# A fused attention and expert kernel: logits of the last pass in twelve products of their own, rows by transposes, two turns moved

## The chip, the cores and the metric

The kernel runs on one core of a Trainium2 chip. Its time is device microseconds (us) of one execution, and what is quoted for a kernel is the median of several. A profiled execution is a further, single one; its trace gives the start and length of every instruction. The engines are TensorE (PE, with its weight loads as PEld), VectorE (DVE), ScalarE (ACT), GpSimd (POOL) and SyncE (SP, which here only issues transfers). Each engine runs its own instructions in the order in which they stand in its queue, and a semaphore holds an instruction until what it needs is there.

## The reference

Three stages follow each other on 1152 tokens (2 batches of 576) of 512 numbers. The first two stages make the tokens that the third one routes:

```python
x = attention_with_rotary(q, k, v)            # 2 x 8 heads x 576 x 64 -> 1152 x 512
h = x @ w_in;  g = h / (1 + exp(-1.702 h));  x = g @ w_out     # d_ff = 2048
logits = x @ w_gate                            # 8 experts
e = argmax(logits);  gate = softmax(logits)[e]
for i in range(1152):                          # slots in order of the tokens
    if counts[e[i]] < capacity: disp[e[i], counts[e[i]]] = x[i]; counts[e[i]] += 1
y = relu(disp @ w1[e]) @ w2[e]                 # F = 1024
out[i] = gate[i] * y[e[i], pos[i]]             # 0 for a token without a slot
```

## The kernel before

**Stages.** Attention comes first and is not touched. What the code calls the first part is the dense layer (`first`, L731): the tokens go through it in three passes of 480, 384 and 288 (`CUTS = 0, 5, 9, 12`, in blocks of 96 tokens, six blocks to a batch). The second part (`second`, L995, and `few`, L1018) is the experts' layer. It works on items: an item is up to 288 tokens of one expert, and a table `etab` says which expert. Items 0 and 1 hold tokens of batch 0 (3 blocks of 96, 2 of 112), items 2 and 3 those of batch 1 (3 of 96, 1 of 96), and for these inputs there are no more.

**Both layers** go through `ffn` (L690): weights arrive in slices, ACT (L672) and DVE (L673) split each into a high and a low part (`hl`, a ring of four buffers), twelve products make the hidden block `h` (L686), ACT and DVE turn it into `gh` and `gl`, and two slices later twelve products add to the output `y` (L712). A `hook` is a pair: a number of slices before the end, and a call to be made there.

**End of a pass of the first part** (L747 to L767). ACT copies `y` to `yt`, in which a column is a token. For each block of 96 tokens two tiles in PSUM are filled by products of `yt` with `turner`, which holds the identity beside the 512 x 8 gate weights: 128 columns of each product are the tokens' rows, 8 are partial logits. DVE copies the rows (L762), adds up the logits (L763, L766), and SP stores the rows in `x2` in DRAM (L767). The six tiles share two buffers of the pool `ps_m`.

**Routing** (`route`, L769) starts when the six blocks of a batch have logits. DVE finds each token's expert, PE counts tokens ahead of each with small products (`rank`, `count`, L815 to L824), DVE makes the slot number of each token (`r_at`, L856), and POOL scatters six lists of 96 entries into `slots` in DRAM (L868). `gather` (L936) then loads an item's entries (`ent`, L940) and gathers its tokens' rows from `x2` (`got`, L945, four buffers). `turn` (L955) transposes the gathered rows on PE (`tg`, L963) into the next item's input `xt`. Results leave with one scatter for each block (`out`, L987), on POOL's queue too.

**Order.** The program order above goes to a scheduler that places instructions by its own estimates; from then on each engine's order is fixed. The wait of one instruction holds up all behind it on its engine.

Of the kernel before, what the change touches and what calls it, by code (L numbers as in the profile page):

```python
# [9 lines left out]
F32 = mybir.dt.float32  # L10
# [14 lines left out]
P = 128  # L25
DM = H * D
ND = DM // P
N = B * S
DFF = 2048
E = 8  # L30
F2 = 1024
TT = 96
NT = S // TT
# [54 lines left out]
CUTS = 0, 5, 9, 12  # L88
# [505 lines left out]
class Experts:  # L594
# [137 lines left out]
    def first(self, k0, k1, hook=None):  # L732

        nc = self.nc
        nf = DFF // P

        def get(f):
            w = self.weights
            if f not in self.seen and f >= EARLY:
                for u in w.units(f):  # L740
                    u()
            self.seen.add(f)
            return self.halves(w.f[f])

        w = (k1 - k0) * TT
        y = self.ffn(self.xt[:, :, :, k0 * TT:k1 * TT], [lambda f=f: get(f) for f in range(nf)], self.gated, hook)
        yt = self.two.tile([P, ND, WIDE], F32, name="yt", bufs=1)  # L747
        for j in range(ND):
            nc.scalar.activation(out=yt[:, j, 0:w], in_=y[j][:, 0:w], func=AF.Copy)
        for k in range(k0, k1):  # L750
            b, i = divmod(k, NT)
            cs = slice((k - k0) * TT, (k - k0 + 1) * TT)
            row = self.three.tile([P, DM], F32, name="row")[0:TT]
            lg = self.three.tile([TT, 2, E], F32, name="lg", bufs=2)
            for n in range(2):
                t = self.ps_m.tile([P, 2, P + E], F32, tag="m", name="tr")
                for j in range(2):
                    nc.tensor.matmul(  # L758
                        t[0:TT, j], yt[:, 2 * n + j, cs], self.turner[:, 2 * n + j], start=True, stop=True
                    )  # L760
                out = row[:, n * 2 * P:(n + 1) * 2 * P].rearrange("p (j c) -> p j c", j=2)
                nc.vector.tensor_copy(out=out, in_=t[0:TT, :, 0:P])  # L762
                nc.vector.tensor_reduce(  # L763
                    out=lg[:, n], in_=t[0:TT, :, P:].rearrange("p j e -> p e j"), axis=AX.X, op=ALU.add
                )
            nc.vector.tensor_tensor(out=self.logits[b][:, i, :], in0=lg[:, 0], in1=lg[:, 1], op=ALU.add)  # L766
            nc.sync.dma_start(out=self.x2[b][i * TT:(i + 1) * TT, :], in_=row)  # L767

    def route(self, b, L):  # L769
# [66 lines left out]
        tt(sq, sq, items.unsqueeze(1).to_broadcast(wide), ALU.mult)  # L836
        red(base, sq)
        ts(at0, base, float(HALF), ALU.mult, float(first), ALU.add)
        red(ni, items)

# [212 lines left out]
    def run(self):  # L1053
        nc, tc = self.nc, self.tc
        sp = [mybir.EngineType.SP]
        found, x = {}, {}

        def turn(i):
            x[i] = self.turn(found[i][1], i)

        self.logits = [self.two.tile([TT, NT, E], F32, name=f"logits{b}", bufs=1) for b in range(B)]
        for n, (k0, k1) in enumerate(zip(CUTS, CUTS[1:])):
            self.first(k0, k1, {0: (10, self.setup), len(CUTS) - 2: (0, lambda: turn(0))}.get(n))
            if n == 0:
                self.clear()
            for b in range(B):
                if k0 < (b + 1) * NT <= k1:
                    self.route(b, self.logits[b])
                    for k in range(2 * b, 2 * b + 2):
                        found[k] = self.gather(k, [b], *STATIC[k])  # L1070
        for i in range(3):
            self.second(found[i][0], x[i], self.expert(i, sp), ((2, 0, 2)[i], lambda: turn(i + 1)))
        self.few(found[3][0], x[3], self.expert(3, sp))
        n = nc.values_load(self.etab[0:1, ITEMS:ITEMS + 1], min_val=4, max_val=ITEMS)
        with tc.For_i(4, n, 1) as i:
            ent, rows = self.gather(i, [0, 1])
            self.cut = []
            self.second(ent, self.turn(rows, 0), self.expert(i, sp))
# [30 lines left out]
```

## Time and profile before

| | us |
|---|---|
| median of 3 runs | 509.21 (508.87 to 510.66) |
| profiled execution | 510.11 |
| its span, first to last instruction | 508.3 |
| TensorE busy in the span | 469.7 (92%) |
| VectorE / ScalarE / GpSimd busy | 366.7 / 271.6 / 115.0 |
| mean granted TensorE clock | 0.983 |

Times inside a trace are counted from the span's start. The clock is a share of full speed; its two levels are 0.5 (1.2 GHz) and 1 (2.4 GHz), and a stretch's figure is a mean over it. A long share of busy time says little on where a microsecond could be saved: for that one looks for stretches in which the busiest engine stands still, and for what ended them.

### The profile page before, as it was taken

How to read it: one execution, taken by the hardware profiler on the slowest of the kernel's cores; microseconds unless marked ns; L12 is line 12 of the kernel's file. 1: busy time of each engine (PE TensorE's matmuls, PEld its weight loads, DVE VectorE, ACT ScalarE, POOL GpSimd, SP SyncE). 2: the span in 40 equal slices, each digit the busy share in tenths (PEclk: the TensorE clock that was granted, in tenths of full speed). 3: DMA queues.
4: the chain of work that ended last, by engine and by line, in shares of the span. 5: the costliest groups of instructions: out<-in, count | busy, mean ns of one | idle time of the engine just before them, and what ended most of it. 6: DMA issues, size and time to landing. Idle time of an engine off the chain costs nothing.

```text
span 508.3 us, 8728 instructions
## 1 busy us (share of the span) xinstructions
PE 469.7 (92%) x3206; PEld 421.6 (83%) x3206; DVE 366.7 (72%) x746; ACT 271.6 (53%) x514; POOL 115.0 (23%) x117
## 2 busy tenths in 40 slices
PE   1789999998999999999999999999999999499992
PEld 1777687687787778788899999999999999499991
DVE  6798999888788998999835534457856689355570
ACT  3577686676565733534563444466566455254640
POOL 5965633422211200000000000000444025601020
PEclk9999999999999999999999999999999999699997
DMA  7032322330224357574101240001076436735410
GB/s 256 1 100 75 99 77 74 99 80 26 53 64 155 105 187 254 188 265 177 41 1 31 63 170 1 0 11 55 2 250 206 132 125 195 246 97 191 162 50 14
DMA packets 20125, 55.63 MB, mean 109 GB/s; under 512 B 3685, under 2 KB 4869, under 8 KB 20080
## 3 DMA queue, kind: packets, MB, share of 16 engines
q1 hardware_dynamic: 17920, 50.91, 31.3%
q0 software_dynamic: 1728, 3.62, 2.4%
q8 instruction: 27, 0.44, 0.4%
q10 hardware_dynamic: 432, 0.51, 0.3%
q14 instruction: 18, 0.15, 0.1%
HBM read 43.86 MB, written 6.66 MB: 99 GB/s over the span
## 4 chain that ended last, share of the span: by engine, by line
PE 61%; DVE 16%; DMA 10%; issue 5%; ACT 4%; POOL 1%; SPq 0%; POOLq 0%; DVEq 0%; ACTq 0%
PE h L686 22%; PE y L712 20%; PE s L393 6%; PE pv L493 4%; DMA qx<-qs 3%; PE tp L442 3%; DVE nm L397 2%; DMA raw<-in_w_out 2%; PE tr L758 2%; DMA raw<-in_w_in 2%; DVE hl L298 2%; ACT pp L404 1%; DVE m L588 1%; DMA got<-x,ent 1%; POOL slots L868 1%
## 5 line engine op out<-in xcount | busy, mean ns | idle before, releaser
L686 PE MATMUL h<-xt,hl 128*128 128x288 f32 (+4 forms) x960 | 175.2, 322 | 1.2 <-DVE hl L673 1.2
L686 PEld LDWEIGHTS h<-xt,hl 128*128 128x128 f32 x960 | 149.0, 191 | 10.2 <-DVE hl L673 2.8
L673 DVE TENSOR_TENSOR hl<-wf,hl 128x1024 fp32r<-128x1024 f32 x80 | 97.5, 1223 | 53.6 <-ACT hl L672 53.4
L712 PE MATMUL y<-gh,hl 128*128 128x288 f32 (+3 forms) x576 | 126.0, 324 | 0.0
L672 ACT ACTIVATE hl<-wf 128x1024 fp32r<-128x1024 f32 x80 | 84.3, 1058 | 52.5 <-PE y L712 25.5
L712 PEld LDWEIGHTS y<-gh,hl 128*128 128x128 f32 x576 | 96.2, 190 | 3.9 <-ACT gh L722 0.4
L712 PE MATMUL y<-gl,hl 128*128 128x288 f32 (+3 forms) x288 | 78.1, 321 | 0.0
L868 POOL DMA_INDIRECT slots<-entry,r_at x12 | 16.5, 1375 | 207.6 <-ACT hl L672 176.8
L397 DVE TENSOR_REDUCE nm<-s 128x1 f32<-128x576 f32 x72 | 53.8, 752 | 12.3 <-PE s L393 10.9
L404 ACT ACTIVATE pp<-s,nm 128x576 f32<-128x576 f32 x64 | 47.7, 745 | 22.7 <-DVE nm L397 22.4
L721 ACT ACTIVATE g<-h 128x480 f32<-128x480 f32 (+2 forms) x48 | 23.5, 492 | 62.6 <-PE h L686 53.2
L393 PE MATMUL s<-ks,qs 128*128 128x288 f32 (+1 forms) x168 | 53.0, 333 | 1.7 <-ACT pp L404 1.3
L712 PEld LDWEIGHTS y<-gl,hl 128*128 128x128 f32 x288 | 51.2, 188 | 1.8
L393 PE MATMUL s<-ks,qx 128*128 128x288 f32 (+1 forms) x168 | 47.0, 306 | 3.4 <-DMA qx<-qs 2.6
L723 DVE TENSOR_TENSOR gl<-g,gh 128x480 fp32r<-128x480 f32 (+2 forms) x48 | 26.5, 554 | 25.1 <-ACT gh L722 24.3
L212 ACT ACTIVATE pt<-tp 128x512 f32<-128x512 f32 x56 | 33.3, 600 | 20.5 <-PE tp L442 20.0
L442 PE MATMUL tp<-ident,pp 128*128 128x128 f32 x256 | 39.8, 281 | 0.5 <-DVE ptr L214 0.5
L493 PE MATMUL pv<-pt,vr 128*64 128x288 f32 x256 | 39.1, 414 | 0.5 <-DVE pt L214 0.3
L393 PEld LDWEIGHTS s<-ks,qs 128*128 128x128 f32 x168 | 32.7, 196 | 7.8 <-issue 3.5
L393 PEld LDWEIGHTS s<-ks,qx 128*128 128x128 f32 x168 | 32.9, 197 | 4.8 <-issue 2.0
L442 PEld LDWEIGHTS tp<-ident,pp 128*128 128x128 f32 x256 | 30.5, 143 | 5.3 <-issue 2.6
L329 PE MATMUL tq<-ident_r,hl 128*128 128x128 f32 x144 | 18.7, 264 | 14.1 <-DVE hl L298 13.5
(178 smaller groups left out, 580.4 us busy)
## 6 DMA issues: line engine op xcount, KB each, us to landing
wf<-in_w SPq DMA_DIRECT2D x32, 512.0 KB, 4.1
raw<-in_w_in SPq DMA_DIRECT2D x16, 512.0 KB, 4.0
raw<-in_w_out SPq DMA_DIRECT2D x16, 512.0 KB, 4.0
qx<-qs SPq DMA_DIRECT2D x14, 320.0 KB, 4.3
qk<-in_qk SPq DMA_DIRECT2D x12, 288.0 KB, 3.2
vr<-in_v SPq DMA_DIRECT2D x8, 320.0 KB, 5.6
x<-row SPq DMA_DIRECT2D x12, 192.0 KB, 2.1
out<-zero SPq DMA_DIRECT2D x9, 256.0 KB, 3.0
```

What stands on the lines that cost most here:

```text
L212: return e.activation(out=out, in_=x, func=AF.Copy, **({} if scale is None else {"scale": scale}))
L393: nc.tensor.matmul(ps[:, n, c:c + w], x, ks[:, src:src + w], start=j == 0, stop=j == len(mine) - 1)
L397: nc.vector.tensor_reduce(out=nm, in_=ps[:, :, 0:HALF], axis=AX.XY, op=ALU.max, negate=True)
L404: nc.scalar.activation(out=out.rearrange("p (n k) -> p n k", n=2), in_=ps[:, :, 0:HALF], func=AF.Exp, bias=d["nm"][:, i:i + 1], accum_out= ...
L442: nc.tensor.transpose(t[:, kt], pp[:, h, h * 64 + kt * P:h * 64 + (kt + 1) * P], self.ident)
L493: nc.tensor.matmul(o[h * 64:h * 64 + 64], x, y, start=j < 2, stop=j > 7)
L672: nc.scalar.activation(out=hl[:, 0], in_=t, func=AF.Copy)
L673: self.last = nc.vector.tensor_tensor(out=hl[:, 1], in0=t, in1=hl[:, 0].bitcast(F32), op=ALU.subtract).ins
L686: self.nc.tensor.matmul(h, u, v, start=m == 0, stop=m == len(ops) - 1)
L712: nc.tensor.matmul(y[j][:, 0:w], u, v, start=f == LAG and m == 0, stop=f == n + LAG - 1 and m == 2)
L721: nc.scalar.activation(out=g, in_=h, func=AF.Gelu_apprx_sigmoid)
L723: nc.vector.tensor_tensor(out=gl, in0=g, in1=gh.bitcast(F32), op=ALU.subtract)
```

## The change

In the last pass of the first part the logits are made first and apart: three blocks times four products of `yt` with the 8 gate columns alone, summed in PSUM in one tile `lt`, and one copy brings 96 x 24 logits to their place. The rows are then made by plain transposes against the identity, four to a tile, so that three tiles (not six) go through `ps_m`, each with one copy of 96 x 512. The first two passes keep the old form. Besides, the hooks of items 0 and 2 carry 4 where they carried 2: `ffn` makes the call at `f == n - hook[0]`, so the rows for the next item (1 and 3 as the code counts, the second and fourth) are turned at slice 4 of 8 instead of slice 6, which in the program is two slices sooner.

```diff
--- before.py
+++ after.py
@@ -747,10 +747,29 @@
         yt = self.two.tile([P, ND, WIDE], F32, name="yt", bufs=1)
         for j in range(ND):
             nc.scalar.activation(out=yt[:, j, 0:w], in_=y[j][:, 0:w], func=AF.Copy)
+        last = k1 == CUTS[-1]
+        if last:
+
+            n, t = k1 - k0, self.ps_m.tile([P, 512], F32, tag="m", name="lt")
+            t = t[0:TT, 0:n * E].rearrange("p (n e) -> p n e", e=E)
+            for k in range(n):
+                for j in range(ND):
+                    cs = slice(k * TT, (k + 1) * TT)
+                    nc.tensor.matmul(
+                        t[:, k], yt[:, j, cs], self.turner[:, j, P:], start=j == 0, stop=j == ND - 1
+                    )
+            nc.vector.tensor_copy(out=self.logits[1][:, NT - n:], in_=t)
         for k in range(k0, k1):
             b, i = divmod(k, NT)
             cs = slice((k - k0) * TT, (k - k0 + 1) * TT)
             row = self.three.tile([P, DM], F32, name="row")[0:TT]
+            if last:
+                t = self.ps_m.tile([P, 512], F32, tag="m", name="tr")
+                for j in range(ND):
+                    nc.tensor.transpose(t[0:TT, j * P:(j + 1) * P], yt[:, j, cs], self.cst["ident"])
+                nc.vector.tensor_copy(out=row, in_=t[0:TT, :])
+                nc.sync.dma_start(out=self.x2[b][i * TT:(i + 1) * TT, :], in_=row)
+                continue
             lg = self.three.tile([TT, 2, E], F32, name="lg", bufs=2)
             for n in range(2):
                 t = self.ps_m.tile([P, 2, P + E], F32, tag="m", name="tr")
@@ -1069,7 +1088,7 @@
                     for k in range(2 * b, 2 * b + 2):
                         found[k] = self.gather(k, [b], *STATIC[k])
         for i in range(3):
-            self.second(found[i][0], x[i], self.expert(i, sp), ((2, 0, 2)[i], lambda: turn(i + 1)))
+            self.second(found[i][0], x[i], self.expert(i, sp), ((4, 0, 4)[i], lambda: turn(i + 1)))
         self.few(found[3][0], x[3], self.expert(3, sp))
         n = nc.values_load(self.etab[0:1, ITEMS:ITEMS + 1], min_val=4, max_val=ITEMS)
         with tc.For_i(4, n, 1) as i:
```

On TensorE, from the first product that reads the last pass's `yt`, the kernel before has (`tr` is a tile of rows and partial logits, `h` and `y` are item 0's):

```order
L758 MATMUL tr<-turner,yt 96x136 x3
L686 MATMUL h<-xt,hl 128x288 x17
L758 MATMUL tr<-turner,yt 96x136
L686 MATMUL h<-xt,hl 128x288 x2
L758 MATMUL tr<-turner,yt 96x136 x2
```

At the same place, down to the first of the routing's products, the changed kernel has (`lt` holds logits, `tr` rows):

```order
L758 MATMUL lt<-turner,yt 96x8 x3
L769 MATMUL tr<-ident,yt 96x128 x3
L686 MATMUL h<-xt,hl 128x288 x16
L758 MATMUL lt<-turner,yt 96x8 x9
L769 MATMUL tr<-ident,yt 96x128
L686 MATMUL h<-xt,hl 128x288 x18
...
L769 MATMUL tr<-ident,yt 96x128 x4
...
L686 MATMUL h<-xt,hl 128x288 x12
L712 MATMUL y_4554<-gh,hl 128x288 x2
L834 LDWEIGHTS before
L834 MATMUL rank<-r_oh,before 96x2x8
```

The last product for logits now stands 16 `h` products behind the first; before, the last two of the twelve products stood 46 `h` and 13 `y` products behind the first. Left out above are 12 `y` products, among which the last eight transposes stand.

On VectorE the kernel before comes to the routing of batch 1 like this (`lg` partial logits, `r_mx` to `r_s` steps of the routing):

```order
L762 COPY row<-tr 96x256
L763 TENSOR_REDUCE lg<-tr 96x8
L766 TENSOR_TENSOR logits_2206<-lg 96x8
L789 TENSOR_REDUCE r_mx<-logits_2206 96x6
L782 TENSOR_TENSOR r_sc<-logits_2206,r_mx 96x48
```

The changed kernel comes to it like this:

```order
L728 SCALAR_TENSOR_TENSOR gl<-h,gh 128x288
L761 COPY logits_2206<-lt 96x24
L770 COPY row<-tr 96x512
L808 TENSOR_REDUCE r_mx<-logits_2206 96x6
...
L827 CAST r_s_4390<-r_s_4389 96x16
...
L770 COPY row<-tr 96x512 x2
L673 TENSOR_TENSOR hl<-wf,hl 128x1024
L728 SCALAR_TENSOR_TENSOR gl<-h,gh 128x288
L801 TENSOR_TENSOR r_far<-rank,r_left 96x48
```

Six copies and nine additions of logits stood ahead of the routing; now one copy of logits and one of rows do, and the other two copies of rows stand between its first half and `r_far`.

On GpSimd the kernel before has, behind the second routing's scatters (`x6` is `slots`, `out` the results of item 0):

```order
L868 DMA slots<-entry_4461,r_at 5760x4 x6
L940 DMA ent<-slots 96x3x4
L940 DMA ent<-slots 96x4
L987 DMA out<-row,ent 1152x512 x2
L945 DMA got<-x_2193,ent 96x512 x4
L987 DMA out<-row,ent 1152x512 x7
```

The changed kernel has there:

```order
L887 DMA slots<-entry_4457,r_at 5760x4 x6
L959 DMA ent<-slots 96x3x4
L959 DMA ent<-slots 96x4
L964 DMA got<-x_2193,ent 96x512 x4
L1006 DMA out<-row,ent 1152x512 x9
```

The four gathers of items 2 and 3 now stand ahead of all scatters of results. The transposes of the gathered rows of item 2 on TensorE have the same neighbours in both kernels.

## Rows read from the trace of the kernel before

**Rows 1.** The page, 40 slices of 12.7 us: the TensorE clock granted, in tenths.

```profile
PEclk9999999999999999999999999999999999699997
```

**Rows 2.** TensorE's waits from 388 to 508: total us, times, longest.

```profile
PE tg L963 <- DMA got<-x,ent: 6.6, 1, 6.6
```

**Rows 3.** Windows: PE, PEld, DVE, ACT, POOL busy (count), granted clock, DMA share, GB/s.

```profile
430.00:434.60 4.60, 4.57 (x41) 4.39 (x40) 3.73 (x8) 2.81 (x4) 3.85 (x4) 1.00 0.63 162
434.60:441.20 6.60, 0.03 (x1) 0.06 (x1) 1.23 (x1) 1.06 (x1) 5.08 (x6) 0.67 0.95 316
441.20:444.00 2.80, 2.80 (x14) 2.80 (x15) 0.56 (x1) 0.49 (x1) 0.37 (x1) 0.50 0.83 222
444.00:446.00 2.00, 2.00 (x11) 2.00 (x11) 0.39 (x1) 0.36 (x1) 0.00 (x0) 0.50 0.05 18
446.00:448.00 2.00, 2.00 (x15) 2.00 (x15) 0.00 (x0) 0.07 (x1) 0.00 (x0) 0.72 0.00 0
```

**Rows 4.** Chain that ended last, 415 to 442: start us, length us, step.

```profile
415.74 0.17 DVE r_at L856
...
425.12 4.73 DMA slots<-entry,r_at
...
430.14 3.46 DMA ent<-slots
...
435.36 5.68 DMA got<-x,ent
...
441.18 0.87 PE tg L963 x4
```

**Rows 5.** Timeline of POOL: start us, length us, instruction, [idle before, releaser].

```profile
362.36 2.02 POOL L868 DMA_INDIRECT slots<-entry,r_at  x1 [176.80 <-ACT hl L672]
...
380.18 1.15 POOL L945 DMA_INDIRECT got<-x,ent  x1 [1.48 <-DMA ent<-slots]
...
416.19 0.97 POOL L868 DMA_INDIRECT slots<-entry,r_at  x1 [27.74 <-DVE r_ends L782]
...
431.73 1.80 POOL L987 DMA_INDIRECT out<-row,ent  x1 [0.30 <-issue]
...
435.36 1.01 POOL L945 DMA_INDIRECT got<-x,ent  x1 [0.30 <-issue]
```

**Rows 6.** Timeline of TensorE, 392 to 399 and 483 to 484.

```profile
392.02 2.49 PE L686 MATMUL h<-xt,hl 128*128 128x288 f32 x17
394.35 0.40 PE L758 MATMUL tr<-turner,yt 128*96 128x136 f32 x2
...
397.81 0.62 PE L758 MATMUL tr<-turner,yt 128*96 128x136 f32 x4
398.18 0.38 PE L686 MATMUL h<-xt,hl 128*128 128x288 f32 x1
...
483.39 0.62 PE L1012 MATMUL tr<-ident,yt 128*96 128x128 f32 x4
483.77 0.29 PE L686 MATMUL h<-xt,hl 128*128 128x96 f32 x1
```

**Rows 7.** Instructions on tile tr, 388 to 508: durations min/median/max ns, first and last start.

```profile
L758 PE MATMUL tr<-turner,yt x24: 278/279/353, 391.2 to 401.9; 128*96 128x136 f32 x24
```

**Rows 8.** Timeline of DVE, ACT and PE around the routing of batch 1.

```profile
403.12 0.16 DVE L766 TENSOR_TENSOR logits<-lg 96x8 f32<-96x8 f32 x1
...
404.70 1.28 ACT L859 ACT_TABLE_LOAD   x1
...
406.74 0.17 DVE L808 CAST r_s<-r_s 96x16 bf16<-96x16 f32 x1
...
409.40 0.28 PE L815 MATMUL rank<-r_oh,before 96*96 96x16 bf16 x3
...
409.58 0.19 PE L824 MATMUL count<-r_s,ones 96*96 96x8 bf16 x1
...
409.76 0.20 DVE L782 TENSOR_TENSOR r_far<-rank,r_left 96x48 f32<-96x48 f32 x1 [0.56 <-PE count L824]
```

## The prediction

> **What bounds the kernel now.** I read the granted clock over the whole span first: it is full but for two slices near 440 and the very last one, after the work [rows 1]. The waits of TensorE say why: from 388 to the end it stands still once, for 6.6 us, before the transposes of item 2's gathered rows, and the releaser is the gather [rows 2]. The windows price this. TensorE is full up to 434.6 at clock 1.00, does nothing until 441.2, and then runs at 0.50, 0.50 and 0.72 over stretches of 2.8, 2.0 and 2.0 us [rows 3]. Against full speed that loses 1.40 + 1.00 + 0.56 = 3.0 us, so the stop costs 6.6 + 3.0 = 9.6 us. Since TensorE works without a pause on both sides of it, a us of TensorE work added or taken elsewhere in the tail is a us of time.
>
> What is waited for is read in the chain that ended last and on GpSimd's timeline. The logits of the last block are done at 403.28; `r_far`, the first step behind the token count, starts at 409.76 [rows 8]; `r_at` ends at 415.91 [rows 4]; the scatters start at 416.19, two scatters of item 0's results at 431.73 stand between the load of entries (430.14) and the first gather (435.36) [rows 4, 5], which lands 5.68 us later, and TensorE goes on at 441.18 [rows 4].
>
> **The change part by part.** *TensorE's own work.* The trace shows 24 rows for the twelve old products [rows 7], so each is two passes; four passes take 0.37 us (397.81 to 398.18), or 0.0925 each, and 24 take 2.2 us [rows 6]. The transposes of results are one row each, four in 0.38 us (483.39 to 483.77) [rows 6], so twelve cost 1.1. The twelve narrow logits products are shown by no row. They too should be two passes. From below, three `rank` products and one of `ones` take 0.18 us, or 0.045 each [rows 8]; from above, the old products took 0.0925. So they cost 1.1 to 2.2 us; I take 2.2, because the old product loads the same 128 x 96 part of `yt`. They cannot cost less than nothing. Net: -2.2 + 1.1 + 2.2 = +1.1 us (0 to +1.1).
>
> *The logits.* The first product that reads `yt` started at 391.2 [rows 7]. Now six passes and three transposes stand there (0.6 + 0.3, and some 0.3 of waiting for `yt`'s copies), 16 hidden products at 0.137 (17 take 2.33, from 392.02 to 394.35 [rows 6]) = 2.2, and 18 passes = 1.7. That is 396.3, and with one copy about 396.5 instead of 403.28: 6.8 us sooner.
>
> *From the logits to `r_far`.* Behind the last logits product TensorE has one transpose, 18 hidden products, 12 products for `y` with eight transposes among them, 12 hidden and 2 more for `y`, before `rank`: 44 at 0.134 to 0.137 = 6.0, 9 at 0.095 = 0.9. It comes there at about 403.0; `rank` and `count` take about 0.8, and `r_far` starts at about 403.8, not 409.76: 6.0 sooner. VectorE should be ready for it. Before, it needed from 403.28 to 406.91 for the steps up to the last cast, a 1.28 us table load of ScalarE and a weight slice included [rows 8]; from 396.5 that gives 400.1, plus a row copy, about 400.8, ahead of 403.0. Of the gain of 6.8 then 0.8 is lost to TensorE's order. If VectorE were late, TensorE would stop with all behind `rank`: ten `y` products of the slice, the next hidden block, and the turn of item 1.
>
> *From `r_far` to the scatters.* 6.15 us before (409.76 to 415.91). The same steps run, with one weight slice, both copies of item 1's turn and one `gl` among them, as before less one `gl`. Those copies wait for transposes that now stand behind 21 products on TensorE. No row shows this order. The least is the same without the slice and the copies, about 3 us, the most perhaps 9, if each hand-over between three engines is late. I take 6.15, the row itself: `r_at` at 409.9, scatters from 410.2.
>
> *From the scatters to the rows.* Before, 13.95 us from the first scatter to the load of entries, 3.7 more until entries are there (3.46 and issue), then the two results' scatters up to 435.36. Those are now behind the gathers: 410.2 + 13.95 + 3.7 = 427.9. The first routing, which had none between, took 380.18 - 362.36 = 17.8 from scatter to gather [rows 5], against 17.65 here. With 5.8 us to land, item 2's rows are there at 433.7, some 7.5 us sooner. From both sides: 431 to 437, by the 3 and the 9 us above.
>
> *Where TensorE stands then.* It would come to those transposes at 434.6 + 1.1 = 435.7. So the rows are there 2 us ahead, the stop is gone, and with it the half clock. What is late next is nothing but TensorE's own queue.
>
> *Costed at nothing.* VectorE's fewer small steps, since it is not waited for in this stretch. The turn of item 1 two slices sooner: its gathers began at 380.18 [rows 5], some 26 us ahead of its new place. It also frees the gather's buffers, which item 2's third row needs at about 430. The turn of item 3 sooner: it only stands elsewhere among item 2's products. On SP two reads of `etab` now stand ahead of item 1's last weight slice; weights are asked for six slices ahead, and no weight wait shows on TensorE [rows 2]. Without that cover each us late there is a us of time. The results of item 0, now behind the gathers on GpSimd, are waited for by nobody before the end.
>
> *Sum.* -6.6 - 3.0 + 1.1 = -8.5 us. The profiled execution took 510.11, 508.3 of it span, and would come to 501.6. It lies 0.9 above the median of the runs, 509.21; from that the same sum gives 500.7, which is what I predict.
>
> One rule of the Trainium skill speaks against the change: "TensorE: Matmul & The Clock Gate", Part 4 (PE-mode transpose), holds that transposes do not count as a busy TensorE to the clock gate in the way matmuls do. In this trace eight transposes among products near 484 leave the clock at its full level [rows 1, 6], so I give the rule little; the sum by the trace is -8.5.
>
> **The rivals.** *A part of the stop stays.* If rows land at 437 to 439 the stop is 1.3 to 3.3 us, and the clock may fall again, up to the 3.0 of before: 502 to 507. For it: the timetable leaves 2 us, and the step from `r_far` is shown by no row. Against: the lost results' scatters are sure, and the first routing agrees.
>
> *The clock falls at the transposes.* Twelve transposes now stand where matmuls stood, and if TensorE lost its full clock there, once, as behind the stop [rows 3], that would cost about 3.0 us: 503.7. Against: the transposes near 484.
>
> *The change does not do what it says.* The routing starts sooner, but `r_at` does not: VectorE's steps wait in order behind the turn's copies, these behind TensorE's. With `r_at` 6 us later than I have it, as before, the rows are there at 439.7: a stop of 4.0 (TensorE comes 1.1 later, and the gathers 1.5 sooner by the results' scatters), with its 3.0 of clock. 4.0 + 3.0 + 1.1 for 9.6 gives 507.7, no change.
>
> *Slower.* The same knot, tighter: item 1's turn, now nearer to the routing on all three engines, holds VectorE's last steps up, and `r_at` comes later than before. It decides from 419.9 on, 10 us behind my timetable and 4 behind before: rows at 443.7 make a stop of 8.0, and 8.0 + 3.0 + 1.1 for 9.6 is 511.7; with 4 us more it is 515.7. For it: three engines in strict order hand over to each other there. Against: before, the same steps with the same neighbours stopped TensorE nowhere [rows 2].
>
> **How the numbers follow.** My forecast has 0.64, a remaining stop 0.19, the clock at the transposes 0.03, no change 0.08, slower 0.06. Half a per cent, 2.5 us, is about what a measurement of this kernel can tell from no change. Faster holds the first three: 0.86; same 0.08; slower 0.06. The likeliest case's own range is 499.0 to 502.5: narrow logits products at their lower bound give 499.6, and runs of one kernel lie up to 1.5 apart. With the milder half of the remaining stop and the clock case the range for 8 in 10 is 499.0 to 505.0.
>
> **What would show it.** Right: no wait on the gather in TensorE's list, the clock full in all slices up to the end, the last logits copy near 396.5, `r_far` near 403.8, the scatters from about 410, the gathers at once behind the entries, near 428, and TensorE at item 2's transposes near 435.7. The narrow products' spacing settles the +1.1. Wrong would be a wait at `rank` or at item 1's turn, scatters after 413, or a wait on the gather that is still over 2 us.

## The result, and the profile after

The changed kernel took 500.25 us (median of 4 runs, 499.47 to 502.51), the kernel before beside it 509.28 (4 runs, 508.87 to 510.66): a ratio of 0.984 with a 95% interval of 0.981 to 0.986, or 9.0 us less, where 8.5 less (500.7) was forecast. The profiled execution of the changed kernel took 499.47 us, its span is 497.8.

The clock first, as in [rows 1]: 40 slices, in tenths, of the kernel after.

```profile
PEclk9999999999999999999999999999999999999997
```

The slice around 440 (432 to 445) that stood at 6 is full again. The windows of the same kernel behind the turn of item 1 answer to [rows 3], in the same columns (busy us and count of PE, PEld, DVE, ACT, POOL, then the granted clock, DMA share, GB/s):

```profile
430.00:433.00 3.00, 3.00 (x29) 3.00 (x28) 2.17 (x2) 1.89 (x3) 2.39 (x3) 1.00 0.95 298
433.00:436.00 3.00, 3.00 (x30) 3.00 (x29) 1.84 (x4) 1.79 (x3) 2.01 (x2) 1.00 0.90 273
436.00:440.00 4.00, 4.00 (x39) 4.00 (x39) 2.23 (x4) 1.91 (x3) 0.00 (x0) 1.00 0.82 320
440.00:445.00 5.00, 5.00 (x47) 5.00 (x45) 3.90 (x6) 4.26 (x9) 0.00 (x0) 1.00 0.49 153
```

TensorE is busy in all of each, so the wait of [rows 2] has no successor. Its timeline at the changed place and at item 2's rows (start, length, instruction):

```profile
389.78 0.88 PE L758 MATMUL lt<-turner,yt 128*96 128x8 f32 x6
390.51 0.51 PE L769 MATMUL tr<-ident,yt 128*96 128x128 f32 x3
390.77 2.35 PE L686 MATMUL h<-xt,hl 128*128 128x288 f32 x16
392.97 1.62 PE L758 MATMUL lt<-turner,yt 128*96 128x8 f32 x18
394.44 0.29 PE L769 MATMUL tr<-ident,yt 128*96 128x128 f32 x1
...
433.45 0.50 PE L982 MATMUL tg<-ident,got 96*128 96x96 f32 x4
```

The first product that reads `yt` starts at 389.8, and started at 391.2 before [rows 7]: this execution was 1.4 us ahead before anything changed (up to there TensorE's queue holds the same products in the same order in both kernels), so 1.4 has to be added where a start is compared. From that product to item 2's transposes TensorE takes 433.45 - 389.78 = 43.67 us; before, from 391.2 to the stop at 434.6 [rows 3, 7], 43.4. All the new products together cost 0.3 us.

The chain that TensorE waited for, on VectorE (logits, `r_far`, `r_at`) and on GpSimd (first scatter, load of entries, first gather, first scatter of results), answers to [rows 4, 5, 8]:

```profile
394.62 0.18 DVE L761 COPY logits<-lt 96x24 f32<-96x24 f32 x1 [1.21 <-PE lt L758]
...
402.21 0.19 DVE L801 TENSOR_TENSOR r_far<-rank,r_left 96x48 f32<-96x48 f32 x1
...
408.09 0.17 DVE L875 CAST r_at<-r_lin 96x6 int32<-96x6 f32 x1
```

```profile
408.54 0.97 POOL L887 DMA_INDIRECT slots<-entry,r_at  x1 [21.51 <-DVE r_ends L801]
...
419.87 1.29 POOL L959 DMA_DIRECT2D ent<-slots  x2 [3.13 <-DMA slots<-entry,r_at]
425.04 1.02 POOL L964 DMA_INDIRECT got<-x,ent  x1 [3.89 <-PE h L686]
...
431.03 1.54 POOL L1006 DMA_INDIRECT out<-row,ent  x1 [0.31 <-issue]
```

With the 1.4 added, `r_far` stands at 403.6 (forecast 403.8), the first scatter at 409.9 (410.2), the first gather at 426.4 (427.9), item 2's transposes at 434.9 (435.7). Those transposes and what follows them are paced at the full clock again.

### The profile page after: what moved, and what is told of

The parts are those of the page before. It is cut to its first block, busy times and chain, and to the rows that moved or that the text cites. A ratio compares the mean times of both kernels' runs of the same rounds, so it can differ in the third digit from the quotient of the medians.

```text
span 497.8 us, 8726 instructions
## 1 busy us (share of the span) xinstructions
PE 466.6 (94%) x3218; PEld 419.4 (84%) x3218; DVE 364.9 (73%) x735; ACT 271.5 (55%) x514; POOL 116.6 (23%) x117
## 4 chain that ended last, share of the span: by engine, by line
PE 58%; DVE 15%; issue 12%; DMA 6%; ACT 4%; POOL 3%; SPq 0%; POOLq 0%; ACTq 0%; DVEq 0%
PE h L686 20%; PE y L712 19%; PE s L393 7%; PE pv L493 4%; DMA qx<-qs 3%; PE tp L442 3%; DVE nm L397 2%; POOL out L1006 2%; PE tr L777 2%; DVE hl L298 2%; DMA raw<-in_w_in 2%; DVE m L588 1%; ACT pp L404 1%; DVE wf L589 1%; DVE r L416 1%
## 5 line engine op out<-in xcount | busy, mean ns | idle before, releaser
L686 PE MATMUL h<-xt,hl 128*128 128x288 f32 (+4 forms) x960 | 172.2, 318 | 0.2 <-DVE hl L673 0.2
L686 PEld LDWEIGHTS h<-xt,hl 128*128 128x128 f32 x960 | 147.4, 189 | 8.1 <-DVE hl L673 1.0
L712 PE MATMUL y<-gh,hl 128*128 128x288 f32 (+3 forms) x576 | 124.2, 322 | 0.0
L712 PEld LDWEIGHTS y<-gh,hl 128*128 128x128 f32 x576 | 95.1, 188 | 4.0 <-ACT gh L722 0.5
L887 POOL DMA_INDIRECT slots<-entry,r_at x12 | 15.1, 1257 | 199.7 <-ACT hl L672 175.2
L721 ACT ACTIVATE g<-h 128x480 f32<-128x480 f32 (+2 forms) x48 | 23.4, 491 | 62.6 <-PE h L686 53.1
```

Source lines behind the costliest of these rows:

```text
L686: self.nc.tensor.matmul(h, u, v, start=m == 0, stop=m == len(ops) - 1)
L712: nc.tensor.matmul(y[j][:, 0:w], u, v, start=f == LAG and m == 0, stop=f == n + LAG - 1 and m == 2)
L721: nc.scalar.activation(out=g, in_=h, func=AF.Gelu_apprx_sigmoid)
```

## The experiments

All runs stand beside runs of the kernel before; a lone "after" is the changed kernel's 500.25. A narrow product is one with the 8 gate columns alone, a wide one an old one of 136 columns. Either is two passes on TensorE: 24 rows for twelve products, above and in [rows 7].

**The logits alone.** The changed kernel with the rows of items 2 and 4 turned where they were.

```
-  (4, 0, 4)[i]
+  (2, 0, 2)[i]
```

> The change without its hooks: logits first and rows by transposes, but items 1 and 3 turned at slice 6 as before. Theory A (the earlier logits bring item 2's rows sooner, that takes the stop of TensorE and its half clock away; the hooks are worth nothing): 500 to 501.5 us, ratio 0.982 to 0.985, no wait of TensorE on the gather. Rival B (the turn of item 1, moved away from item 2's, does a good part of it by clearing VectorE's last routing steps and the gather's buffers): 503 or more, with a wait on the gather of over 2 us.

500.12 us (499.75 to 500.41), ratio 0.983 (0.980 to 0.987). There is no wait on the gather, and TensorE comes to item 2's rows at 433.97. The new last pass is the whole gain. Item 1's turn does move here: its transposes start at 408.8 to 410.8, and at 405.2 to 405.9 in the changed kernel.

**The hooks alone.** The kernel before with only the hooks moved, (2, 0, 2) to (4, 0, 4).

> The kernel before with the hooks 4, 0, 4 alone. Theory A: no change, ratio 0.998 to 1.002, the wait on the gather still 6 to 7 us and the half clock behind it. Rival B: 506 or less, with a wait on the gather under 4 us.

509.91 us (508.03 to 511.63, 10 runs), ratio 1.002 (1.000 to 1.004). TensorE's wait and two windows:

```profile
PE tg L963 <- DMA got<-x,ent: 5.9, 1, 5.9
```

```profile
440.00:445.00 5.00, 3.06 (x16) 3.09 (x16) 0.56 (x1) 0.49 (x1) 2.45 (x3) 0.53 0.85 261
445.00:450.00 5.00, 5.00 (x38) 5.00 (x38) 0.92 (x3) 1.77 (x3) 0.00 (x0) 0.79 0.01 5
```

The stop and the half clock stand as before. But this run moved only half of what it names: the scheduler left item 1's transposes at the same place in TensorE's queue as in the kernel before, and only those of the fourth item came sooner. That moving item 1's turn is worth nothing is shown by the run of the logits alone, not by this one.

**Logits first, rows as they were.** The narrow products stay in front, and the rows come by the old wide products.

```
-  for j in range(ND): nc.tensor.transpose(t[0:TT, j*P:(j+1)*P], yt[:, j, cs], ident)
+  for n in range(2): for j in range(2):
+      nc.tensor.matmul(t[0:TT, j], yt[:, 2*n+j, cs], self.turner[:, 2*n+j], start=True, stop=True)
```

> The changed kernel with logits first in narrow products, but the last pass's rows still made by the old wide products (136 columns, two passes each, six tiles and six copies). Theory A: what counts is that logits come first; the old rows cost TensorE 24 passes of 0.0925 for 12 transposes of 0.09 to 0.095, so 1.1 us more than the change: 501 to 502.5 us, and item 2's rows 2 to 3 us later than in the change, still no stop or one under 1 us. Rival E (the plain transposes, with half the tiles and copies, are what frees the way): a wait on the gather of over 3 us and 504 or more.

502.06 us (501.94 to 502.31), ratio 0.987 (0.984 to 0.991), no wait on the gather. So the earlier logits remove the stop, and the plain transposes are worth only their TensorE time. That prices the products.

```profile
390.61 0.87 PE L758 MATMUL lt<-turner,yt 128*96 128x8 f32 x6
...
435.81 0.50 PE L986 MATMUL tg<-ident,got 96*128 96x96 f32 x4
```

From the first product on `yt` (390.61) to item 2's transposes (435.81) it takes 45.2 us; before, 43.4. The difference is 24 narrow passes: 1.8 / 24 = 0.075 us each, not the 0.0925 of the sum. And 45.2 - 43.67 = 1.53 is 24 wide passes less twelve transposes at 0.095 [rows 6]: (1.53 + 1.14) / 24 = 0.111 for a wide pass, more than the 0.0925 of the sum. With 0.108 for a transpose, as the doubled run below has it, it is 0.118.

**The wait moved, not the chain.** The kernel before, with the first transposes of item 2's rows held until the last hidden block of item 1 is through, 58 products later.

```
+  self.late = the last product of a hidden block          # in words
+  add_manual_dep(transpose, self.late, NoSync)            # for item 2's rows
```

> The kernel before, with no change to logits or routing: only the transposes of item 2's rows are pinned in TensorE's queue behind the last hidden block of item 1, 58 products later than before. Theory A, in its full form (the stop is there because these transposes stand in a strict queue ahead of some 7 us of work that is ready): the stop shrinks from 6.6 to 1 us or less, the clock stays full, 500.5 to 502 us, ratio 0.983 to 0.986, without any earlier routing. Rival D (item 2's input itself is late, so the stop only moves on to its first products): 506 to 509 us, a wait of 4 us or more at item 2's transposes or its first hidden block.

505.12 us (503.51 to 508.56, 6 runs), ratio 0.993 (0.989 to 0.997): a miss, by some 4 us, and two fifths of the gain (3.8 of 9.0). The profiled execution took 507.64, one of the slower ones. Its first transposes start without a stop, but the next ones wait, and the clock falls again:

```profile
PE tg L963 <- DMA got<-x,ent: 2.6, 1, 2.6
```

```profile
442.00:445.00 3.00, 0.46 (x5) 0.49 (x6) 1.69 (x2) 1.07 (x2) 0.12 (x1) 1.00 1.03 214
445.00:447.00 2.00, 2.00 (x12) 2.00 (x11) 0.56 (x1) 0.49 (x1) 0.00 (x0) 0.50 1.00 352
447.00:449.00 2.00, 2.00 (x13) 2.00 (x13) 0.27 (x1) 1.19 (x2) 0.00 (x0) 0.65 0.38 147
```

Later places in TensorE's queue hide part of a late chain. The wait then stands at the next rows, and half speed followed 2.6 us of it (1.0 + 0.7 = 1.7 us in these windows). Behind the pinned transposes TensorE also waits 0.8 us for a copy of item 1's results and 0.7 for item 2's input, which it did not before.

**Logits last.** The changed kernel with the narrow products behind the rows' transposes instead of ahead of them.

```
-  if last: (logits)        # ahead of the loop over rows
+  if last: (logits)        # behind it
```

> The changed kernel with the last pass's logits made after its rows in the program, not before: transposes and narrow products as in the change, 12 of each. In TensorE's queue the last narrow product then stands 36 places later and the token count 29 places, 3.9 us, later than in the change. Theory A': it is not being first in itself that matters but getting the routing early enough; rows of item 2 come 3 to 5 us later than in the change, which had some 3.6 us to spare, so a stop of 0 to 1.5 us and 500 to 502.5 us. Rival G (only with the logits ahead of the rows is the stop gone): a wait on the gather of over 3 us and 504 or more.

501.47 us, with a wide spread (499.80 to 506.03, 5 runs), ratio 0.984 (0.981 to 0.987). The profiled execution is the 506.03 one, and it has a stop:

```profile
PE tg L981 <- DMA got<-x,ent: 2.4, 1, 2.4
```

```profile
415.73 0.97 POOL L886 DMA_INDIRECT slots<-entry,r_at  x1 [26.68 <-DVE r_ends L800]
```

Its first scatter is at 415.73, where the changed kernel's is at 408.54; 2.0 of that lie ahead of the last pass (first product on `yt` at 391.8 for 389.8), 5.2 are the order. The median lies in the range of A'; the stop seen lies between what A' and G expected. At that lateness the margin is gone, and I read the spread as executions on either side of it; only the late side was profiled. The scatters' start alone does not decide. With the rows as they were it came nearly as late, 23.4 us behind the first product on `yt` (23.9 here), and there was no stop: from the first scatter to the landing of the first gathered rows it took 17.7 us there, 22.4 here and 21.3 in the changed kernel. Why this stretch varies stays open.

All 24 narrow passes stand in a row here (399.15 to 401.28), and the granted clock behind them is 1.00.

**How much margin there is.** The changed kernel with ten small GpSimd copies between `r_at` and the scatters. The queues of TensorE, VectorE and ScalarE are in the same order as in the changed kernel. On GpSimd one scatter of item 0's results now also stands ahead of the first gather (428.26, 0.97 us long), which it does not hold up: GpSimd is idle for 2.85 us between the two.

```
+  held = tile([TT, 20, NT])
+  10 x nc.gpsimd.tensor_copy(out=held, in_=at (broadcast))
-  scatter by at        +  scatter by held[:, 19]
```

> The changed kernel with ten GpSimd copies of the slot numbers (96 x 120 each) put between r_at and the second routing's scatters; all other queues are in the same order. They should take 3 to 5 us. Theory A: the gather's first rows land about 3.6 us before TensorE comes to them, so the first 3.6 us cost nothing, and what is over costs its length and some half clock: 500 to 502.5 us, with a wait on the gather equal to the delay less 3.6. Rival F (the routing's length itself is on the path, through the later steps it releases): 503 to 505.5, a us for a us.

505.00 us (504.85 to 505.34), ratio 0.992 (0.990 to 0.995). GpSimd's copies with the scatter behind them, TensorE at item 2's rows, and the windows from there:

```profile
409.20 7.17 POOL L890 COPY held<-r_at 96x120 int32<-96x120 int32 x10 [21.30 <-DVE r_ends L801]
416.82 0.97 POOL L893 DMA_INDIRECT slots<-entry,held  x1 [0.46 <-POOL held L890]
```

```profile
437.10 0.52 PE L988 MATMUL tg<-ident,got 96*128 96x96 f32 x4 [2.63 <-DMA got<-x,ent]
```

```profile
437.10:438.00 0.90, 0.90 (x8) 0.90 (x9) 0.00 (x0) 0.34 (x1) 0.60 (x2) 0.87 0.97 341
438.00:440.00 2.00, 2.00 (x12) 2.00 (x11) 0.60 (x2) 0.51 (x2) 1.70 (x2) 0.50 1.01 283
440.00:441.20 1.20, 1.20 (x7) 1.20 (x7) 0.35 (x1) 0.00 (x0) 0.18 (x1) 0.51 1.00 393
```

The copies took 7.6 us up to the scatter, not the 3 to 5 expected, for which no row stood, and brought back a stop of 2.63 us with half clock behind it (0.12 + 1.0 + 0.59 = 1.7): 4.3 of the 4.75 us over after. So lateness of the scatters alone brings the stop back. The time lies in the range of rival F, but not by its reason: a us for a us would be 7.6, not 4.75. The gather's landing moved less than the scatter: 425.04 to 432.08 for its first issue is 7.0, of which 0.9 is this execution's later start (390.65 for 389.78 at the changed place). So 6.1 us of delay made 2.6 of stop, and the rows of the changed kernel land about 3.5 us ahead of TensorE, where the forecast had 2. Its own trace agrees: the first gather lands 4.8 us behind 425.04, at 429.8, and TensorE comes at 433.45.

**The new form in all three passes.**

```
-  last = k1 == CUTS[-1]
+  last = True              # and the copy of the logits split by batch
```

> The changed kernel with the new form (narrow logits products, rows by transposes) in all three passes of the first part, so in nine more blocks. It prices TensorE's passes. By the whole stretch in the traces (a wide pass 0.111 us in its place, a narrow one 0.077, a transpose 0.095) a block costs 8 x 0.077 + 4 x 0.095 - 8 x 0.111 = 0.11 more, 1.0 us in all: 500.5 to 502 us. By the prices of the prediction (0.0925 for a wide and a narrow pass) a block costs 0.38 more, 3.4 us in all: 503 to 504.5.

506.75 us (503.83 to 508.20, 10 runs), ratio 0.995 (0.993 to 0.997): 6.5 us slower than after, outside both expectations. TensorE's rows and clock at the end of the second pass:

```profile
342.01 2.30 PE L758 MATMUL lt<-turner,yt 128*96 128x8 f32 x26
```

```profile
342.00:344.30 2.30, 2.30 (x30) 2.30 (x29) 0.87 (x3) 0.14 (x1) 0.00 (x0) 1.00 0.00 0
344.30:345.10 0.80, 0.80 (x9) 0.80 (x8) 0.76 (x3) 0.00 (x0) 0.00 (x0) 1.00 0.00 0
345.10:348.60 3.50, 3.50 (x18) 3.46 (x17) 2.88 (x12) 2.59 (x4) 0.00 (x0) 0.52 0.22 63
```

TensorE never stands still here, and yet its clock is halved for 3.5 us, just behind a run of 26 narrow passes: 1.7 us lost. Later TensorE waits 1.7 us for item 0's rows (L985, at 387.74). Of the 7.2 us by which the profiled spans differ, these are 3.4; 2.4 lie ahead of the first changed product (268.2 for 265.8), and the 1.4 left are about what the other products cost, where the two expectations had 1.0 and 3.4. So the clock, the forecast's second rival, can fall without a stop, but here it falls behind narrow products, not behind transposes. The last three runs were made for it.

**The gate as weights in all passes.** Four products for the logits of a whole pass, `w_gate` loaded and `yt` moving, then a small transpose for each block.

```
-  nc.tensor.matmul(t[:, k], yt[:, j, cs], self.turner[:, j, P:], ...)     # for each k
+  nc.tensor.matmul(g, self.turner[:, j, :], yt[:, j, 0:w], ...)
+  nc.vector.tensor_copy(out=gt, in_=g)
+  nc.tensor.transpose(t[:, k], gt[:, k*TT:(k+1)*TT], ident)               # for each k
```

> A version meant to beat both: rows by transposes in all passes, and the logits of a whole pass in four products with the 8 gate columns as the weights and yt moving (480, 384 or 288 columns), then turned back by one small transpose for each block. Against the change TensorE loses 72 wide passes (8.0 us) and 24 narrow ones (1.85), and gets 36 transposes (3.4), 12 small ones (about 1.0) and 24 passes of 384 columns in the mean. If such a pass takes a column a cycle these are 3.8 us, net -1.6: 498 to 499.5 us. If it takes two cycles a column, 7.7 us, net +2.2: 502 to 503. No stop in either case unless the routing of batch 1 comes more than 3 us later.

507.16 us (505.81 to 510.02, 10 runs), ratio 0.998 (0.995 to 1.000): meant to beat both kernels, it is 6.9 us slower than after and can hardly be told from the kernel before (508.87 beside it). The logits' products of the second pass, those of the last with its small transposes, and the first scatter:

```profile
340.25 2.75 PE L750 MATMUL lt<-yt,turner 128*8 128x384 f32 x8
...
396.18 1.62 PE L750 MATMUL lt<-yt,turner 128*8 128x288 f32 x6
400.04 0.65 PE L750 MATMUL lt<-yt,turner 128*8 128x288 f32 x2
403.98 0.30 PE L756 MATMUL lb<-ident,gt 8*96 8x8 f32 x3
```

```profile
420.48 0.97 POOL L870 DMA_INDIRECT slots<-entry,r_at  x1 [27.07 <-DVE r_ends L784]
```

The clock held. TensorE's own work is what costs: the passes of 384 columns start 0.32 us apart, where the expectation's first case needs 3.8 / 24 = 0.16 and its second 7.7 / 24 = 0.32, so it is the second. Of the 7.6 us by which the profiled spans differ, 2.2 lie ahead of the first changed product (267.95 for 265.78), 4.2 more are there when the last pass's first product starts (396.18 for 389.78), and 1.2 come behind. The 4.2 are, in the first two passes, 16 moving passes (6.2), 36 transposes (3.4) and nine small ones (0.6) for 72 wide passes (6.6), and a wait of 0.5 for item 0's rows.

The hand-over to VectorE and back puts TensorE's queue between the products and the small transposes: the logits end 8 us behind the start of their products. The scatters come 11.9 us later than after, of which 6.4 are there before the last pass and 5.5 are the hand-over. That uses up the margin, but TensorE waits only 0.4 us for item 2's rows.

**Logits twice.** The changed kernel with its logits products made twice over.

```
-  for k in range(n):
+  for k in 2 * tuple(range(n)):
```

> The changed kernel, with its twelve logit products made twice over (24 further narrow passes in the same tile, the same values written again). Theory A (the small products cost only their passes and leave the clock alone): 24 x 0.077 = 1.8 us more on TensorE, the logits and all behind them 1.8 us later, which is inside the 3.4 us that the delayed scatters showed to be spare; no stop at item 2's rows, granted clock 1.00 throughout, time 500.3 + 1.8 = 502.1 (501.5 to 503). Rival C (a long run of narrow products is itself followed by the half clock, as behind the run of 26 in the second pass of the kernel with the new form everywhere, where TensorE did not wait and yet had 0.50 for some 3.5 us): half clock around 396 to 400, 1.8 us more on TensorE and as much on the logits' chain: 504 to 505.5, with a stop at item 2's rows as the slack is used up.

505.20 us (503.09 to 506.72, 4 runs), ratio 0.990 (0.987 to 0.993). TensorE around the products and at item 2's rows:

```profile
393.36 0.88 PE L758 MATMUL lt<-turner,yt 128*96 128x8 f32 x6
...
396.55 3.74 PE L758 MATMUL lt<-turner,yt 128*96 128x8 f32 x42
...
440.60 0.49 PE L982 MATMUL tg<-ident,got 96*128 96x96 f32 x4
```

```profile
396.50:400.20 3.70, 3.70 (x45) 3.70 (x44) 0.46 (x1) 1.29 (x2) 0.00 (x0) 0.97 0.45 146
400.20:402.80 2.60, 2.60 (x13) 2.60 (x13) 2.40 (x14) 0.65 (x2) 0.00 (x0) 0.50 0.25 69
402.80:406.00 3.20, 3.20 (x25) 3.19 (x25) 1.59 (x6) 0.41 (x1) 0.00 (x0) 0.91 0.03 11
```

Half clock behind the run of 42 passes, with TensorE busy throughout: rival C. From the first product on `yt` (393.36) to item 2's transposes (440.60) it takes 47.24 us, 3.6 more than after: 24 passes at 0.077 (1.8) and the clock (0.1 + 1.3 + 0.3 = 1.7). There is no stop, so on that point rival C missed: the routing was that much later, and so was TensorE. The rest of this profiled execution's lateness lies ahead of the changed place.

**Rows twice.** The same with the last pass's transposes.

```
-  for j in range(ND):
+  for j in 2 * tuple(range(ND)):
```

> The changed kernel, with the twelve transposes of its last pass made twice over (24 further passes, the same values written again). Theory A: 24 x 0.095 = 2.3 us more on TensorE, behind the logits and so mostly beside the routing; no stop, clock 1.00, time 500.3 + 2.3 = 502.6 (502 to 503.5). Rival C for transposes (they do not keep the clock up): half clock between 396 and 402, another 1.5 to 2 us: 504 to 505.

502.24 us (501.90 to 502.51), ratio 0.986 (0.984 to 0.987). The expectation counted two passes for a transpose; it is one, so twelve were added, and that the time lies in the expected range is partly luck. The clock over the span, and TensorE at the changed place and at item 2's rows:

```profile
PEclk9999999999999999999999999999999999999996
```

```profile
391.20 0.86 PE L758 MATMUL lt<-turner,yt 128*96 128x8 f32 x6
...
436.17 0.49 PE L982 MATMUL tg<-ident,got 96*128 96x96 f32 x4
```

No fall: the transposes do not lower it, even doubled. From the first product on `yt` (391.20) to item 2's rows (436.17) it takes 44.97 us, 1.3 more than after, 0.108 a transpose.

**The new form in two passes.** The changed kernel with the second pass in the new form too.

```
-  last = k1 == CUTS[-1]
+  last = k0 > 0            # and the copy of the logits split by batch
```

> The changed kernel with the new form in its second pass as well (four slices, 32 narrow passes and 32 of transposes in place of 32 wide ones), the first pass as it was. If the half clock behind the second pass's run of narrow products, seen once in the kernel with the new form everywhere, belongs to that form (rival C at four slices): granted clock under 0.9 around 343 to 349, TensorE +2.0 (32 x (0.077 + 0.095 - 0.111)) and +1.8 of clock, the item 0 gather later by what is then missing: 503.5 to 505.5. If it was chance, or needs the first pass's form too (theory A): clock 1.00, 502 to 503.

503.38 us (502.07 to 505.37, 4 runs), ratio 0.988 (0.985 to 0.991), between the two expected ranges. The +2.0 for TensorE counted two passes for a transpose again; with one (16, not 32) it is 32 x 0.077 + 16 x 0.095 - 32 x 0.111 = +0.4. The second pass again:

```profile
340.61 2.30 PE L758 MATMUL lt<-turner,yt 128*96 128x8 f32 x26
```

```profile
342.80:346.40 3.60, 3.60 (x18) 3.60 (x18) 2.44 (x12) 1.39 (x2) 0.00 (x0) 0.53 0.19 57
```

The half clock behind 26 narrow passes in a row repeats, for 1.7 us, and needs nothing of the first pass. It is no longer "seen once": runs of 42 and, twice, of 26 were followed by it; the changed kernel's run of 18 was not. But neither were the run of 24 with the logits last, nor one of 34 in the first pass of the kernel with the new form everywhere. So the length of the run alone does not decide, and what does stays open. It may not come in every execution either: the mean granted clock is 0.991 in three of these four and 0.994 in the fastest (502.07), and 0.992 to 0.994 in the changed kernel.

## Why the prediction was right

- **The stop, -6.6: held.** No wait on the gather is left. The new last pass does it without the hooks, and the logits in front do it with the old rows; the delayed scatters bring the stop back with the other engines' queues as they are. What counts is that the logits are early enough: behind the rows' transposes they gave 501.47, with a stop in the execution that was profiled.
- **The half clock, -3.0: held.** The 34 products and transposes from item 2's rows on took 6.55 us before (441.18 to 447.73) and take 3.71 (433.45 to 437.16): 2.8. The page shows the clock low in one slice near 440 and not in two, which changes nothing, as the 3.0 came from the windows.
- **TensorE's own work, +1.1: the mis-sized term.** It measured +0.3. A narrow pass cost 0.075 us by the stretch with the old rows, and in the changed kernel's row of 18 they start 0.085 apart; it is not 0.0925. The wide passes that went away had cost 0.111 to 0.118 in their place. I divided the 0.37 us to the next product's start by four, but the hidden product behind such a run then takes 0.22 us (398.18 to 398.40) where 0.137 is usual, so that some 0.09 of the run's cost stands in it: (0.37 + 0.08) / 4 = 0.113. The 0.095 of a transpose was read in the same way, and the doubled run has 0.108. The bounds of 0 to +1.1 held it.
- **The timetable** was right to 0.3 us up to the scatters. From there the rows came sooner: 11.3 us from the first scatter to the load of entries instead of 13.95, more than the 1.5 lost between entries and gather (5.2 instead of 3.7). The margin was 3.5 us, not 2. The steps from `r_far` to `r_at`, taken at 6.15 from the old row between bounds of 3 and 9, came to 6.05; as no row showed the new order, so close a hit is partly luck. One sum is 0.2 off: 396.3 + 6.0 + 0.9 is 403.2, not 403.0.
- **Hooks at nothing, results behind the gathers at nothing: held.** The first is shown by the run without the hooks; the second only by the result, as it wasn't tried alone. The 26 us given for item 1's gathers belong to the first gather of all (380.18), for item 0; the last of the five, for item 1, starts at 387.20 in that trace, which leaves 19 to the 406.2 meant there, and is still ample.
- **The rivals.** A part of the stop stays: not here, but 6 us more on the chain give it. The clock at the transposes: not so, neither for twelve nor for 24; the Trainium skill's rule in "TensorE: Matmul & The Clock Gate", Part 4, had no effect here (the granted clock is full up to the last slice of the doubled run). But the clock did fall at long runs of the narrow products. I had given the clock 0.03, and for the wrong instruction. The changed kernel's own runs of six and 18 were not followed by it.
- **The sum.** 6.6 + 2.8 - 0.3 = 9.1 us, and the medians differ by 9.0. The profiled spans differ by 10.5; the other 1.4 lie ahead of the change.

## What to carry to other kernels

When a full TensorE stands still once, follow what it waits for back to its first late input, and move that input's producer ahead of its neighbours; shifting the wait in the queue gave two fifths as much. Price such a stop with the clock behind it, and look at the clock also behind runs of tiny products without any wait. Price an operation that goes away by a whole stretch, with the product behind it, not by the next product's start.

## What was not expected of the hardware

- Runs of 26 and 42 narrow passes were followed by half clock, with 1.7 us lost each time, though TensorE never stood idle; runs of 18, 24 and 34 were not.
- Stops of 2.4 us and twice 2.6, and not only of 6.6, were followed by half clock (1.7 us lost behind each); one of 1.7 us was not (the new form in all passes, 1.00 from 385.9 to 396).
- A small GpSimd copy (96 x 120 elements, int32) took 0.72 us.
